# Layer B of a four-layer kernel: one accumulator bank per projection, the output product in four column quarters, the residual store behind the next step's first products

## The chip, the cores and the metric

The kernel runs on one core of one Trainium2 chip. The metric is the device time in microseconds (us) of one execution; "before" and "after" name the two kernels.

Words used throughout: TensorE (PE in the profile) multiplies, and each of its products is preceded by a weight load (PEld); VectorE (DVE), ScalarE (ACT) and GpSimd (POOL) work on elements; PSUM is the accumulator memory, which this program uses as eight banks of 512 float32 columns; SBUF is where the program keeps its other tiles. A *product* is one matmul instruction. Four products on four groups of 32 columns of the array run side by side (in the profile below, 20 products of 512 columns, five times four, take 1.07 us from start to start); I call four such a *round*. A *pass* is one whole output product of a step: 64 products before, 128 after.

## The reference

The program applies layers A, B, A, B to a sequence of 2048 tokens of width 640, each with a layer norm ahead and a residual add behind. Only B is changed. It is a recurrent transformer: 64 segments of 32 tokens, each with 8 memory tokens ahead of it, 32 heads of 128, and the memory of the next segment is the output of this one.

```python
mem = mem0
for s in range(64):
    h = concat([mem, x[:, 32*s : 32*s+32]])            # 8 + 32 tokens, 640 wide
    q, k, v = (einsum('btd,dhe->bhte', h, W) for W in (Wq, Wk, Wv))
    p = softmax(where(mask, q @ k.T * scale, -1e9))    # per head, 40 x 40
    o = einsum('bhte,hed->btd', p @ v, Wo)             # 4096 -> 640
    mem = o[:, :8]                                     # feeds the next segment
    outs.append(o[:, 8:])
```

So 64 steps form a chain: nothing of step s+1 that touches its memory tokens can start before the output product of step s has ended.

## The kernel before

The kernel skews the segments: a step handles rows 0 to 23 of segment s together with the 8 memory tokens of the next one; rows 24 to 31 of four segments (the "tails") are handled together, as filler work, and their output product is "deferred" to step 0 of the next four. So the steps repeat in cycles of four. The transposes between the products' layout (tokens on partitions) and that of the scores (features on partitions) are done by VectorE from PSUM.

The Q and K products of one half of the heads (16 of 32) share a two-bank tile; everything else takes one of four banks of a common pool:

```python
pp  = tile_pool(name="b_ps",  bufs=4, space=PSUM)     # one bank each
pot = tile_pool(name="b_pot", bufs=2, space=PSUM)     # two banks each

def qk(Wt, ps, b, dst):
    thin_mm(ps, cols, Wt, b, w_heads)                 # 5 chunks x 4 products, 512 columns
    tq = turn(ps)                                     # VectorE: 128x512 transpose to SBUF
    place("dve", tq, b, heads(dst[s]), 0, 8, 24)
    ...                                               # cut: GpSimd places the rest
# ... one step:
A_, B_ = pair_tile("b_QKa"), pair_tile("b_QKb")
qk(W.wq, A_[:, 0, :], 0, QT)
qk(W.wk, A_[:, 1, :], 0, KT)
qk(W.wq, B_[:, 0, :], 1, QT)
scores(0)
qk(W.wk, B_[:, 1, :], 1, KT)
...                                                   # cut: sums, normalise, V, values
```

The output product has 320 columns per product; the two halves of the width for two heads fill the four column groups, so the result has to be added across partitions afterwards, twice (for the next state and for the residual). Its end, and the end of the step:

```python
def run(self, k):                                     # class OPass
    if self.ps is None:
        self.ps = ps_tile([128, 320], F32, self.name)
    while k > 0 and self.p < 16:
        for e in range(2):
            h = self.horder[2 * self.p + e]
            for jj2 in range(2):
                q = 2 * e + jj2
                nc.tensor.matmul(self.ps[32*q:32*q+32, :], lhsT=self.src_fn(h),
                                 rhs=W.wo[:, h, 320*jj2:320*jj2+320], tile_position=(0, 32*q), ...)
...
fill(0.66); op.run(4); values(1); ...; op.run(4); fill(0.22); op.run(8)
...
nc.vector.transpose(out=TM, in_=ops[:])               # 128 x 320
for hf in range(2):                                   # two adds give the next state
    nc.vector.tensor_tensor(out=hT[s+1][64*hf:64*hf+64, :, 24:32],
        in0=TM[0:64, hf:10:2, 24:32], in1=TM[64:128, hf:10:2, 24:32], op=ALU.add)
fill(9)                                               # what is left of the filler
xo = add_out(ops, XO, "b_xnb")                        # two adds, 64 x 320, then the store
```

`fill` issues the filler products of the step: the tails (20 products of 512 columns per unit) in steps 1 to 3, the deferred output product in step 0.

Of the kernel before, what the change touches and what calls it, by code (L numbers as in the profile page):

```python
# [18 lines left out]
F32 = mybir.dt.float32  # L19
# [10 lines left out]
NCH = 5  # L30
# [28 lines left out]
def layernorm_tile(nc, pool, C, xt, xn_out, name):  # L59
# [8 lines left out]
    nc.vector.tensor_scalar(out=xn_out.rearrange("p (g jj d) -> p jj g d", jj=2, d=32),  # L68
                            in0=xt.rearrange("p (jj g d) -> p jj g d", jj=2, d=32),
# [497 lines left out]
def load_B_weights(nc, tc, ctx, B_Wq, B_Wk, B_Wv):  # L567
# [4 lines left out]
    for nm, src in (("wq", B_Wq), ("wk", B_Wk), ("wv", B_Wv)):  # L572
        t = wp.tile([128, NCH, 4096], BF16, name=f"b_{nm}")
        setattr(W, nm, t)
        sv = src.rearrange("(jj g d) h e -> g jj d (h e)", jj=2, d=32)
        for c in range(NCH):
            def load(t=t, sv=sv, c=c):
                for q in range(4):
                    nc.sync.dma_start(t[32 * q:32 * q + 32, c, :], sv[2 * c + q // 2, q % 2])
            loads.append(load)  # L580
# [3 lines left out]
def layer_B(nc, tc, C, W, wo_src, x_src, xb_src, x_dst, mem0, general, nsteps=64, out_bf16=False):  # L584
# [6 lines left out]
    with ExitStack() as ctx:  # L591
# [6 lines left out]
        pp = ctx.enter_context(tc.tile_pool(name="b_ps", bufs=4, space=PSUM))  # L598
# [18 lines left out]
        XO = st.tile([64, 320], F32, name="b_XO")  # L617
# [162 lines left out]
        class OPass:  # L780
            def __init__(self, src_fn, horder, name):
                self.src_fn, self.horder, self.name = src_fn, horder, name
# [3 lines left out]
            def run(self, k):  # L786
                if self.ps is None:
                    self.ps = ps_tile([128, 320], F32, self.name)
                while k > 0 and self.p < 16:
                    for e in range(2):  # L790
                        h = self.horder[2 * self.p + e]
                        for jj2 in range(2):
                            q = 2 * e + jj2
                            nc.tensor.matmul(self.ps[32 * q:32 * q + 32, :], lhsT=self.src_fn(h), rhs=W.wo[:, h, 320 * jj2:320 * jj2 + 320],
                                             start=(self.p == 0), stop=(self.p == 15), tile_position=(0, 32 * q), skip_group_check=True)
# [4 lines left out]
        def add_out(ops, XO, name):  # L800

            nc.vector.tensor_tensor(out=XO[0:64, :], in0=ops[0:64, :], in1=XO[0:64, :], op=ALU.add)
            if out_bf16:
                xnb = wk.tile([64, 320], BF16, name=name, tag="xnb")
                nc.vector.tensor_tensor(out=xnb[0:64, :], in0=ops[64:128, :], in1=XO[0:64, :], op=ALU.add)
                return xnb
            nc.vector.tensor_tensor(out=XO[0:64, :], in0=ops[64:128, :], in1=XO[0:64, :], op=ALU.add)
# [9 lines left out]
        for q in range(4):  # L817
# [3 lines left out]
        nc.vector.tensor_copy(m0[:, 1, :].rearrange("p (g jj d) -> p jj g d", jj=2, d=32),  # L821
                              m0[:, 0, :].rearrange("p (jj g d) -> p jj g d", jj=2, d=32))
# [18 lines left out]

        def load_deferred(T_):
            XOd[T_] = wk.tile([64, 320], F32, name="b_XOd", tag="XOd")
            for jj2 in range(2):
                for i in range(4):
                    r = 32 * (4 * T_ + i) + 24
                    nc.sync.dma_start(XOd[T_][32 * jj2 + 8 * i:32 * jj2 + 8 * i + 8, :], x_src[r:r + 8, 320 * jj2:320 * jj2 + 320])

        xn_pending = []
        for s in range(nsteps):  # L850
# [4 lines left out]
            for jj2 in range(2):  # L855
                nc.sync.dma_start(XO[32 * jj2:32 * jj2 + 24, :], x_src[32 * s:32 * s + 24, 320 * jj2:320 * jj2 + 320])
# [62 lines left out]
            def qk(Wt, ps, b, dst):  # L919

                thin_mm(ps, cols, Wt, b, w_heads)
                tq = turn(ps)
# [66 lines left out]
            A_, B_ = pair_tile("b_QKa"), pair_tile("b_QKb")  # L989
            qk(W.wq, A_[:, 0, :], 0, QT)  # L990
            qk(W.wk, A_[:, 1, :], 0, KT)
            qk(W.wq, B_[:, 0, :], 1, QT)
# [3 lines left out]
            qk(W.wk, B_[:, 1, :], 1, KT)  # L996
# [171 lines left out]
```

## Time and profile before

| | before |
|---|---|
| time, median (range) of 4 runs | 2796.89 us (2793.56 to 2800.34) |
| products on TensorE | 54,988, each with a weight load |
| one cycle of four steps in layer B | 62.3 us, 32 of them |
| TensorE's largest wait: first K for the transposed Q | 192.2 us |

The prediction below walks through the profile that leads there. Lines of the page of the kernel before give: busy time, share of the span and number of instructions of each engine; a DMA queue with the number of its packets, MB, and their share of the time of 16 engines; and a group of instructions (out<-in, shape, count | busy us, mean ns of one | idle before, and what ended most of it).

### The profile page before, as it was taken

The page shows a single profiled execution, that of the slowest core. Times are in us where ns is not written, and L with a number is a line of the kernel's source. Part 1 is how long each engine was busy: PE and PEld are TensorE (multiplying, and loading weights), DVE is VectorE, ACT ScalarE, POOL GpSimd, SP SyncE. Part 2 cuts the span into 40 slices and gives each one's busy share as a digit, 9 for nine tenths or more (in the row PEclk, how much of TensorE's full clock was granted, in tenths as well). Part 3 has the DMA queues.
Part 4 walks back from the last instruction along what each step waited for, and adds up shares of the span by engine and source line. Part 5 has one row for each costly group of instructions (what it writes and reads, how often), then busy time and mean ns, then how long its engine had stood idle before and what let it go on. Part 6 is the DMA issues. An engine that isn't in the chain of part 4 may idle for free.

```text
span 2796.9 us, 123979 instructions
## 1 busy us (share of the span) xinstructions
PE 2327.0 (83%) x54988; PEld 1285.9 (46%) x54988; DVE 1753.7 (63%) x4029; ACT 882.6 (32%) x2067; POOL 994.4 (36%) x2333
## 2 busy tenths in 40 slices
PE   6888878888888888888588887888888888888886
PEld 3444444444444444445344443444444444444443
DVE  5666656666666666666556665666666666666665
ACT  4665622222222222222156664222222222222221
POOL 2333433333333333333223433333333333333332
PEclk9988889999999999999889898999999999999999
DMA  6652330000000000000213324000000000000000
GB/s 170 162 150 84 110 96 21 19 21 19 21 22 20 20 20 22 19 18 18 68 55 121 114 81 159 18 17 17 18 18 17 17 18 17 20 18 17 15 16 13
DMA packets 98851, 131.87 MB, mean 47 GB/s; under 512 B 20592, under 2 KB 84096, under 8 KB 96384
## 3 DMA queue, kind: packets, MB, share of 16 engines
q1 hardware_dynamic: 96704, 122.20, 16.0%
q8 instruction: 432, 7.08, 1.1%
q10 hardware_dynamic: 1600, 1.66, 0.2%
q14 instruction: 115, 0.94, 0.1%
HBM read 89.17 MB, written 26.21 MB: 41 GB/s over the span
## 4 chain that ended last, share of the span: by engine, by line
PE 55%; DVE 19%; issue 7%; ACT 5%; DMA 2%; SPq 1%; POOL 1%; DVEq 0%; ACTq 0%; POOLq 0%
PE b_QKb L87 11%; PE b_V L87 10%; DVE b_TQ L87 9%; PE b_OPS L87 9%; PE b_QKa L87 8%; PE b_tail L87 3%; PE a_PP L87 3%; PE b_SP L87 3%; ACT a_PT L87 2%; PE b_OTL L87 2%; ACT b_OTsb L87 1%; PE a_S L87 1%; DVE b_TM L87 1%; ACT b_R L87 1%; DVE b_XO L87 1%
## 5 line engine op out<-in xcount | busy, mean ns | idle before, releaser
L87 PEld LDWEIGHTS <-b_hT 128*32 128x32 bf16 x15520 | 437.0, 98 | 644.6 <-issue 396.5
L87 ACT ACTIVATE b_PT<-b_SP 128x224 bf16<-128x224 f32 x256 | 91.5, 358 | 1098.5 <-PE b_SP L87 1089.7
L87 PE MATMUL b_OPS<-b_wo,b_OTsb 128*32 128x320 bf16 x8192 | 347.4, 301 | 17.2 <-ACT b_OTsb L87 13.1
L87 ACT ACTIVATE a_PT<-a_S 128x768 bf16<-128x768 f32 (+1 forms) x384 | 325.7, 891 | 84.9 <-PE a_S L87 77.9
L87 PE MATMUL b_QKa<-b_wk,b_hT 128*32 128x512 bf16 x2560 | 179.9, 413 | 192.2 <-DVE b_TQ L87 192.2
L87 PE MATMUL b_V<-b_wv,b_hT 128*32 128x512 bf16 x5120 | 325.0, 380 | 0.0
L87 DVE STREAM_TRANSPOSE b_TQ<-b_QKa 128x512 f32<-128x512 f32 x256 | 183.5, 717 | 193.3 <-PE b_QKa L87 190.6
L87 DVE STREAM_TRANSPOSE b_TQ<-b_QKb 128x512 f32<-128x512 f32 x256 | 183.5, 717 | 175.2 <-PE b_SP L87 116.0
L87 POOL CAST b_KT<-b_TQ 128x384 bf16<-128x384 f32 x254 | 142.7, 562 | 421.8 <-DVE b_TQ L87 421.8
L87 PEld LDWEIGHTS <-b_OTsb 128*32 128x32 bf16 x8192 | 187.1, 96 | 138.0 <-ACT b_OTsb L87 72.5
L87 POOL CAST b_QT<-b_TQ 128x384 bf16<-128x384 f32 x254 | 140.8, 554 | 297.4 <-DVE b_TQ L87 297.4
L87 DVE TENSOR_TENSOR b_PT<-b_PT,b_R 128x160 bf16<-128x160 bf16 (+1 forms) x512 | 215.0, 460 | 44.8 <-ACT b_R L87 44.4
L87 POOL TENSOR_TENSOR b_Rtot<-b_Rtot,b_R 128x160 bf16<-128x160 bf16 x256 | 142.8, 558 | 240.1 <-ACT b_R L87 224.5
L87 PE MATMUL b_QKb<-b_wk,b_hT 128*32 128x512 bf16 x2560 | 161.6, 380 | 50.2 <-DVE b_TQ L87 50.2
L87 PE MATMUL b_QKa<-b_wq,b_hT 128*32 128x512 bf16 x2560 | 162.9, 381 | 32.4 <-DVE b_hT L87 32.3
L87 POOL TENSOR_SCALAR_AFFINE_SELECT a_PT<-a_PT 128x256 bf16<-128x256 bf16 x256 | 109.6, 433 | 214.3 <-ACT a_PT L87 203.0
L87 ACT CAST b_OTsb<-b_OTL 128x320 bf16<-128x320 f32 x384 | 148.7, 421 | 114.5 <-PE b_OTL L87 114.4
L87 DVE CAST b_Vsb<-b_V 128x512 bf16<-128x512 f32 x256 | 174.4, 684 | 7.4 <-PE b_V L87 6.4
L87 PE MATMUL b_QKb<-b_wq,b_hT 128*32 128x512 bf16 x2560 | 175.0, 402 | 0.0
L87 PE MATMUL a_PP<-a_xnT,a_wt 128*128 128x512 bf16 x560 | 157.4, 417 | 2.7 <-DVE a_t1k L87 0.9
L87 ACT ACTIVATE b_R<-b_SP 128x160 f32<-128x160 f32 x256 | 78.1, 305 | 232.5 <-PE b_SP L87 232.5
L87 DVE STREAM_TRANSPOSE b_TM<-b_OPS 128x320 f32<-128x320 f32 x126 | 64.8, 514 | 137.4 <-PE b_OPS L87 137.4
(160 smaller groups left out, 3791.1 us busy)
## 6 DMA issues: line engine op xcount, KB each, us to landing
a_wt<-a_wpad SPq DMA_DIRECT2D x112, 160.0 KB
b_wo<-in_B_Wo_dram SPq DMA_DIRECT2D x8, 1280.0 KB
b_Vt<-b_Vtb SPq DMA_DIRECT2D x512, 16.0 KB
b_XO<-xres SPq DMA_DIRECT2D x256, 30.0 KB
a_wvo<-in_A_wo_dram SPq DMA_DIRECT2D x8, 800.0 KB
b_wq<-in_B_Wq_dram SPq DMA_DIRECT2D x20, 256.0 KB
b_wk<-in_B_Wk_dram SPq DMA_DIRECT2D x20, 256.0 KB
xres<-a_xo SPq DMA_DIRECT2D x16, 320.0 KB
```

The source lines that it names most:

```text
L87: r = f(*a, **k)
```

## The change

The intent: let the first products of a step follow each other without waiting for VectorE (a bank for every projection), shorten the chain from the output product to the next state (four column quarters need no add across partitions), and take the residual adds out of the way of the next step's first transpose. To pay for the banks, the common pool goes from four to three and the output product gets a bank of its own. The weights and the layer norm are laid out so that each column group gets one quarter of the width.

```diff
-        pp = tile_pool(name="b_ps", bufs=4, space=PSUM)
+        pp = tile_pool(name="b_ps", bufs=3, space=PSUM)
+        po = tile_pool(name="b_po", bufs=1, space=PSUM)
 class OPass:
-                    self.ps = ps_tile([128, 320], F32, self.name)
+                    self.ps = self.pool.tile([128, 160], F32, name=self.name, tag=self.tag)
-                        for jj2 in range(2):
-                            q = 2 * e + jj2
-                            matmul(self.ps[32*q:32*q+32, :], lhsT=src(h), rhs=W.wo[:, h, 320*jj2:320*jj2+320], ...)
+                        for q in range(4):
+                            matmul(self.ps[32*q:32*q+32, :], lhsT=src(h), rhs=W.wo[:, h, 160*q:160*q+160], ...)
 def add_out(ops, XO, name):                      # XO: [64, 320] -> [128, 160]
-            tensor_tensor(out=XO[0:64, :], in0=ops[0:64, :], in1=XO[0:64, :], op=ALU.add)
-                xnb = wk.tile([64, 320], BF16, name=name, tag="xnb")
-                tensor_tensor(out=xnb[0:64, :], in0=ops[64:128, :], in1=XO[0:64, :], op=ALU.add)
+                xnb = wk.tile([128, 160], BF16, name=name, tag=name)
+                tensor_tensor(out=xnb[:], in0=ops[:], in1=XO[:], op=ALU.add)
 # the step
-            A_, B_ = pair_tile("b_QKa"), pair_tile("b_QKb")
-            qk(W.wq, A_[:, 0, :], 0, QT)
-            qk(W.wk, A_[:, 1, :], 0, KT)
-            qk(W.wq, B_[:, 0, :], 1, QT)
+            qk(W.wq, "b_Qa", 0, QT)              # qk now takes a bank of the pool
+            qk(W.wk, "b_Ka", 0, KT)
+            while late: late.pop(0)()            # adds and stores of the step before
+            ... # cut: loads of the residual rows, moved here
+            qk(W.wq, "b_Qb", 1, QT)
-            fill(0.66)
+            fill(1.0)
             ...
-            fill(0.22)
-                TM = wk.tile([128, 10, 32], F32, ...)
-                for hf in range(2): tensor_tensor(out=hT[s+1][64*hf:...], ..., op=ALU.add)
+                TM = wk.tile([128, 5, 32], F32, ...)
+                tensor_copy(hT[s + 1][:, :, 24:32], TM[:, :, 24:32])
-            xo = add_out(ops, XO, "b_xnb"); ...  # store here
+            late.append(store)                   # the deferred output's store as well
```

Cut from it: the layout of the weights, the memory input and the layer norm's output, and the DMA lists that follow from the quarters.

More of the change, by code (lines that the diff above doesn't have):

```diff
@@ L67, in layernorm_tile @@
     nc.gpsimd.tensor_tensor(out=rstd[:], in0=rstd[:], in1=C.mhalf[:, 0:1], op=ALU.pow)
-    nc.vector.tensor_scalar(out=xn_out.rearrange("p (g jj d) -> p jj g d", jj=2, d=32),
-                            in0=xt.rearrange("p (jj g d) -> p jj g d", jj=2, d=32),
+    nc.vector.tensor_scalar(out=xn_out.rearrange("p (g q d) -> p q g d", q=4, d=32),
+                            in0=xt.rearrange("p (q g d) -> p q g d", q=4, d=32),
                             scalar1=mv[:, 0:1], scalar2=rstd[:, 0:1], op0=ALU.subtract, op1=ALU.mult)
@@ L574, in load_B_weights @@
         setattr(W, nm, t)
-        sv = src.rearrange("(jj g d) h e -> g jj d (h e)", jj=2, d=32)
+        sv = src.rearrange("(q g d) h e -> g q d (h e)", q=4, d=32)
         for c in range(NCH):
@@ L578, in load @@
                 for q in range(4):
-                    nc.sync.dma_start(t[32 * q:32 * q + 32, c, :], sv[2 * c + q // 2, q % 2])
+                    nc.sync.dma_start(t[32 * q:32 * q + 32, c, :], sv[c, q])
             loads.append(load)
@@ L597, in layer_B @@
         W.wo = wop.tile([128, 32, D], BF16, name="b_wo")
-        pp = ctx.enter_context(tc.tile_pool(name="b_ps", bufs=4, space=PSUM))
+        pp = ctx.enter_context(tc.tile_pool(name="b_ps", bufs=3, space=PSUM))
+        po = ctx.enter_context(tc.tile_pool(name="b_po", bufs=1, space=PSUM))
         pot = ctx.enter_context(tc.tile_pool(name="b_pot", bufs=2, space=PSUM))
@@ L616, in layer_B @@
             nc.vector.memset(Rtot[:], 0.0)
-        XO = st.tile([64, 320], F32, name="b_XO")
+        XO = st.tile([128, 160], F32, name="b_XO")
         nc.vector.memset(XO[:], 0.0)
@@ L780, in layer_B, with __init__ @@
         class OPass:
-            def __init__(self, src_fn, horder, name):
-                self.src_fn, self.horder, self.name = src_fn, horder, name
+            def __init__(self, src_fn, horder, name, pool=pp, tag="ps"):
+                self.src_fn, self.horder, self.name, self.pool, self.tag = src_fn, horder, name, pool, tag
                 self.ps = None
@@ L791, in run @@
                         h = self.horder[2 * self.p + e]
-                        for jj2 in range(2):
-                            q = 2 * e + jj2
-                            nc.tensor.matmul(self.ps[32 * q:32 * q + 32, :], lhsT=self.src_fn(h), rhs=W.wo[:, h, 320 * jj2:320 * jj2 + 320],
-                                             start=(self.p == 0), stop=(self.p == 15), tile_position=(0, 32 * q), skip_group_check=True)
+                        for q in range(4):
+                            nc.tensor.matmul(self.ps[32 * q:32 * q + 32, :], lhsT=self.src_fn(h), rhs=W.wo[:, h, 160 * q:160 * q + 160],
+                                             start=(self.p == 0 and e == 0), stop=(self.p == 15 and e == 1),
+                                             tile_position=(0, 32 * q), skip_group_check=True)
                     self.p += 1
@@ L800, in add_out @@
         def add_out(ops, XO, name):
-            nc.vector.tensor_tensor(out=XO[0:64, :], in0=ops[0:64, :], in1=XO[0:64, :], op=ALU.add)
             if out_bf16:
-                xnb = wk.tile([64, 320], BF16, name=name, tag="xnb")
-                nc.vector.tensor_tensor(out=xnb[0:64, :], in0=ops[64:128, :], in1=XO[0:64, :], op=ALU.add)
+                xnb = wk.tile([128, 160], BF16, name=name, tag=name)
+                nc.vector.tensor_tensor(out=xnb[:], in0=ops[:], in1=XO[:], op=ALU.add)
                 return xnb
-            nc.vector.tensor_tensor(out=XO[0:64, :], in0=ops[64:128, :], in1=XO[0:64, :], op=ALU.add)
+            nc.vector.tensor_tensor(out=XO[:], in0=ops[:], in1=XO[:], op=ALU.add)
             return XO
@@ L820, in layer_B @@
         alloc_h(0)
-        nc.vector.tensor_copy(m0[:, 1, :].rearrange("p (g jj d) -> p jj g d", jj=2, d=32),
-                              m0[:, 0, :].rearrange("p (jj g d) -> p jj g d", jj=2, d=32))
+        nc.vector.tensor_copy(m0[:, 1, :].rearrange("p (g q d) -> p q g d", q=4, d=32),
+                              m0[:, 0, :].rearrange("p (q g d) -> p q g d", q=4, d=32))
         mt = ps_tile([128, NCH, 8], BF16, "b_m0T")
@@ L840, in layer_B, with deferred_rows @@
         XOd = {}
+        def deferred_rows(x, T_, q):
+            v = x.rearrange("(t i k) d -> t i k d", i=4, k=32)
+            return v[T_, :, 24:32, 160 * q:160 * q + 160]
         def load_deferred(T_):
-            XOd[T_] = wk.tile([64, 320], F32, name="b_XOd", tag="XOd")
-            for jj2 in range(2):
-                for i in range(4):
-                    r = 32 * (4 * T_ + i) + 24
-                    nc.sync.dma_start(XOd[T_][32 * jj2 + 8 * i:32 * jj2 + 8 * i + 8, :], x_src[r:r + 8, 320 * jj2:320 * jj2 + 320])
+            XOd[T_] = wk.tile([128, 160], F32, name="b_XOd", tag="XOd")
+            for q in range(4):
+                nc.sync.dma_start(XOd[T_][32 * q:32 * q + 32, :], deferred_rows(x_src, T_, q))
         xn_pending = []
+        late = []
         for s in range(nsteps):
@@ L854, in layer_B @@
                 load_deferred(T - 1)
-            for jj2 in range(2):
-                nc.sync.dma_start(XO[32 * jj2:32 * jj2 + 24, :], x_src[32 * s:32 * s + 24, 320 * jj2:320 * jj2 + 320])
             if not last:
@@ L917, in row_max, with qk @@
                 mrows.append(mr)
-            def qk(Wt, ps, b, dst):
+            def qk(Wt, name, b, dst):
+                ps = ps_tile([128, 512], F32, name)
                 thin_mm(ps, cols, Wt, b, w_heads)
-                tq = turn(ps)
+                tq = turn(ps[:])
                 place("dve", tq, b, heads(dst[s]), 0, 8, 24)
@@ L987, in take, with vpass @@
                 evac(eng, OTsb[:, h:h + 8, :].rearrange("p (j r) c -> p j (r c)", j=2), OTL[b, jp][:, :, 0:160])
-            A_, B_ = pair_tile("b_QKa"), pair_tile("b_QKb")
-            qk(W.wq, A_[:, 0, :], 0, QT)
-            qk(W.wk, A_[:, 1, :], 0, KT)
-            qk(W.wq, B_[:, 0, :], 1, QT)
+            def vpass(b):
+                V = ps_tile([128, 512], F32, "b_V")
+                thin_mm(V, vcols, W.wv, b, w_cols)
+                evac("dve", Vsb[:, b, :], V[:])
+            qk(W.wq, "b_Qa", 0, QT)
+            qk(W.wk, "b_Ka", 0, KT)
+            while late:
+                late.pop(0)()
+            for q in range(4):
+                nc.sync.dma_start(XO[32 * q:32 * q + 24, :], x_src[32 * s:32 * s + 24, 160 * q:160 * q + 160])
+            qk(W.wq, "b_Qb", 1, QT)
             if general:
@@ L995, in layer_B @@
             scores(0)
-            qk(W.wk, B_[:, 1, :], 1, KT)
+            qk(W.wk, "b_Kb", 1, KT)
             while xn_pending:
@@ L1004, in layer_B @@
                 row_max(1)
-            Va = ps_tile([128, 512], F32, "b_V")
-            thin_mm(Va, vcols, W.wv, 0, w_cols)
-            evac("dve", Vsb[:, 0, :], Va[:])
+            vpass(0)
             scores(1)
-            Vb = ps_tile([128, 512], F32, "b_V")
-            thin_mm(Vb, vcols, W.wv, 1, w_cols)
-            evac("dve", Vsb[:, 1, :], Vb[:])
+            vpass(1)
             sums(1)
@@ L1018, in layer_B @@
                 tails_to_seg(s + 1)
-            fill(0.66)
-            op = OPass(lambda h: OTsb[:, h, 0:32], HORDER, "b_OPS")
+            fill(1.0)
+            op = OPass(lambda h: OTsb[:, h, 0:32], HORDER, "b_OPS", po, "op")
             op.run(4)
@@ L1041, in layer_B @@
             if not last:
-                TM = wk.tile([128, 10, 32], F32, name="b_TM", tag="TM")
+                TM = wk.tile([128, NCH, 32], F32, name="b_TM", tag="TM")
                 nc.vector.transpose(out=TM[:].rearrange("p g t -> p (g t)"), in_=ops[:])
-                for hf in range(2):
-                    nc.vector.tensor_tensor(out=hT[s + 1][64 * hf:64 * hf + 64, :, 24:32], in0=TM[0:64, hf:10:2, 24:32],
-                                            in1=TM[64:128, hf:10:2, 24:32], op=ALU.add)
+                nc.vector.tensor_copy(hT[s + 1][:, :, 24:32], TM[:, :, 24:32])
             fill(9)
@@ L1051, in layer_B, with store @@
                 ln_dma((s + 7) // 4)
-            xo = add_out(ops, XO, "b_xnb")
-            for jj2 in range(2):
-                nc.sync.dma_start(x_dst[32 * s:32 * s + 24, 320 * jj2:320 * jj2 + 320], xo[32 * jj2:32 * jj2 + 24, :])
+            def store(s=s, ops=ops):
+                xo = add_out(ops, XO, "b_xnb")
+                for q in range(4):
+                    nc.sync.dma_start(x_dst[32 * s:32 * s + 24, 160 * q:160 * q + 160], xo[32 * q:32 * q + 24, :])
+            late.append(store)
             def store_deferred(T_, od):
@@ L1059, in store_deferred @@
                 xd = add_out(od.ps, XOd.pop(T_), "b_xnbd")
-                for i in range(4):
-                    for jj2 in range(2):
-                        r = 32 * (4 * T_ + i) + 24
-                        nc.sync.dma_start(x_dst[r:r + 8, 320 * jj2:320 * jj2 + 320], xd[32 * jj2 + 8 * i:32 * jj2 + 8 * i + 8, :])
+                for q in range(4):
+                    nc.sync.dma_start(deferred_rows(x_dst, T_, q), xd[32 * q:32 * q + 32, :])
             for u in units:
                 if isinstance(u, OPass):
-                    store_deferred(T - 1, u)
+                    late.append(lambda u=u, T=T: store_deferred(T - 1, u))
             if last:
+                while late:
+                    late.pop(0)()
                 od = deferred.pop(T)
```

## The prediction

(Cut from the text, each cut marked: rules of the hardware that did not come from this case's traces. No term of the sum goes with them: 2796 - 214 - 22 - 20 = 2540 us still stands, on times of the trace before. Without them the 69 ns of a round of 160 columns is an estimate from that trace: 512 columns in 214 ns scale to 67, the 224 columns of b_blk in 0.10 us to 71. Measured later: 69 ns in the kernel after; a round of 320 columns, 135.5 in the text, takes 136 before. That makes 2.21 us per pass against 2.18, so the 0.04 per step, 0.2 in the sum of a cycle, is as fine as these readings go. That Q can be transposed while K's products run was the author's reading, not shown by the trace before; the kernel after shows it, see "Right" below.)

> **What bounds the kernel now.** I first read the page. Its chain of waits puts over half of the span on TensorE and a fifth on VectorE, nearly all in layer B (tiles b_...), and part 5 names the largest wait of TensorE: 192.2 us ahead of the K product of the first half of the heads, until VectorE's transposed copy b_TQ is done. Both products lie in one two-bank tile, b_QKa.
>
> ```profile
> PE 55%; DVE 19%; issue 7%; ACT 5%; DMA 2%; SPq 1%; POOL 1%; DVEq 0%; ACTq 0%; POOLq 0%
> ...
> L87 PE MATMUL b_OPS<-b_wo,b_OTsb 128*32 128x320 bf16 x8192 | 347.4, 301 | 17.2 <-ACT b_OTsb L87 13.1
> ...
> L87 PE MATMUL b_QKa<-b_wk,b_hT 128*32 128x512 bf16 x2560 | 179.9, 413 | 192.2 <-DVE b_TQ L87 192.2
> ...
> L87 PE MATMUL b_QKb<-b_wk,b_hT 128*32 128x512 bf16 x2560 | 161.6, 380 | 50.2 <-DVE b_TQ L87 50.2
> ```
>
> Layer B runs 64 steps, twice. The starts of the Q product in the timeline repeat every four steps (0: the filler is the deferred output product; 1, 2, 3: V, Q, K tails; a layer norm ends step 2, its transposes lie in step 3). So I asked for the stretches of one cycle:
>
> ```profile
> 813.68:829.23 15.55, 13.26 (x404) 8.07 (x404) 10.33 (x23) 3.25 (x11) 6.71 (x16) 1.00 0.07 17
> 829.23:844.39 15.16, 13.31 (x385) 7.38 (x373) 10.01 (x23) 3.83 (x12) 5.89 (x15) 1.00 0.12 27
> 844.39:860.12 15.73, 13.43 (x380) 7.44 (x377) 10.87 (x26) 3.83 (x12) 5.06 (x11) 1.00 0.07 16
> 860.12:876.00 15.88, 13.76 (x381) 7.53 (x382) 10.12 (x23) 3.84 (x12) 5.63 (x12) 1.00 0.10 24
> sum 62.32, PE 53.76 PEld 30.42 DVE 41.33 ACT 14.75 POOL 23.28; mean PE 13.44 PEld 7.61 DVE 10.33 ACT 3.69 POOL 5.82
> ```
>
> Columns: length, then busy TensorE, weight loads, VectorE, ScalarE, GpSimd, granted clock. No engine fills a step; VectorE is at two thirds. TensorE is the in-order path, and its holes make the step. Its timeline at the head of step 1:
>
> ```profile
> 829.23 1.25 PE L87 MATMUL b_QKa<-b_wq,b_hT 128*32 128x512 bf16 x20
> 831.83 1.26 PE L87 MATMUL b_QKa<-b_wk,b_hT 128*32 128x512 bf16 x20 [1.34 <-DVE b_TQ L87]
> 832.90 1.26 PE L87 MATMUL b_QKb<-b_wq,b_hT 128*32 128x512 bf16 x20
> 833.98 0.26 PE L87 MATMUL b_SP<-b_mask,c_identb 128*32 128x160 bf16 x4
> 834.33 0.37 PE L87 MATMUL b_SP<-b_QT,b_KT 128*32 128x40 bf16 x32
> 835.06 1.26 PE L87 MATMUL b_QKb<-b_wk,b_hT 128*32 128x512 bf16 x20 [0.36 <-DVE b_TQ L87]
> 836.13 0.29 PE L87 MATMUL b_SP<-b_PT,b_blk 128*32 128x160 bf16 x8
> 836.23 1.27 PE L87 MATMUL b_V<-b_wv,b_hT 128*32 128x512 bf16 x20
> ```
>
> Unblocked, a product starts 1.07 us after its predecessor (831.83 to 832.90). Before the first K there are 2.60 - 1.07 = 1.5 us of hole. VectorE starts a transpose 1.38 us after a product starts, if it is free; here it first does the output adds of the last step, so Q is transposed only at 831.06.
>
> The second layer B has one thing more, in step 1. VectorE's timeline there:
>
> ```profile
> 2089.71 0.48 DVE L87 TENSOR_TENSOR b_XOd<-b_OPSd,b_XOd 64x320 f32<-64x320 f32 x1
> 2091.57 0.49 DVE L87 TENSOR_TENSOR b_xnbd<-b_OPSd,b_XOd 64x320 bf16<-64x320 f32 x1 [1.38 <-DMA out_dram<-b_xnb]
> 2092.09 0.72 DVE L87 STREAM_TRANSPOSE b_TQ<-b_QKa 128x512 f32<-128x512 f32 x1
> ```
>
> The two output tiles share one buffer, so the add waits for a store and the Q transpose waits behind it.
>
> [...] Q and K lie in different banks of the pair, so I read the 1.5 us as a wait of the tile's bookkeeping, not of the chip; this kernel never overlaps the two, so its trace cannot show it. [...] 20 products of 512 columns in 1.07 us are 5 rounds of 214 ns. [...] the window 2092.86 to 2096.27, behind a hole of 2.9 us, has a granted clock of 0.59. [...] The row-sum products b_blk (one round of 160 columns, one of 64) take 0.10 us (836.13 to 836.23)[...]. So 160-column rounds should stream at about 69 ns.
>
> **The change part by part.**
> Own banks: the first K starts behind Q. Holes removed in steps 0 to 3, from starts in the timeline less 1.08 us: 1.81, 1.52, 1.07, 1.82 = 6.2. The second K needs no transpose any more either: 0.5 us per step (835.06 - 834.33 - 0.22 for the scores), 2.0 per cycle. Sum 8.2.
>
> Scores of the first half still need K transposed and placed: K starts at 1.08, transpose at 2.46 to 3.18, cast (0.23) to 3.44, scores at 3.6, against 3.3 when TensorE could: 0.3, as now.
>
> Output product in quarters: 128 products instead of 64, half as long: 32 x 69 = 2.21 us against 16 x 135.5 = 2.17. Cost 0.04 per step.
>
> The chain to the next step gets shorter: transpose 128x320 (517 ns; 512 columns take 717, so some 1.05 ns per column) becomes 128x160, about 350; two adds of 196 become one copy of about 200. So 0.35 less. Outside step 2 the five filler rounds left (1.08 us) cover the chain (estimate 0.9 us) and nothing is gained; in step 2 the layer norm makes VectorE late and the gain is about 0.4.
>
> Filler moved forward: the first output product now waits 0.25 us for b_OTsb (step 2); two more filler parts (0.43) cover it. Gain 0.25 per step, 1.0 per cycle. But the filler part before the last output products is gone, and b_OTsb comes 1.06 us after the values start while 0.84 of work is left: loss 0.22 per step, 0.9 per cycle.
>
> Store moved behind K: adds of 4 x 0.48 us at worst leave the Q transpose's way and become one of about 0.33 (two in step 1), in front of the transpose of the second Q.
>
> Three single banks instead of four: I took from the built program which instruction each bank wait names. Two of them bite. In step 3 the first V waits for the transpose of the second K, since the layer norm's transposes took a bank: about 0.7. In step 1 the second K waits for the deferred add: about 0.4. The values wait for V's copy, which starts behind normalising: about 0.2 more per step, 0.8 per cycle.
>
> Sum per cycle: 8.2 + 1.0 + 0.4 gained; 0.2 + 0.9 + 0.7 + 0.4 + 0.8 lost: 6.6. Laying the instructions of each step one after another by hand gives 13.4, 13.75, 14.3, 14.1, together 55.6 against 62.3, so 6.7. Times 32 cycles: 214 us.
>
> Second layer B, step 1: 16.5 instead of 15.15 us where the clock stays up, because of the shared buffer; the names are separate now: 16 x 1.35 = 22 us. The slow-clock windows add to the steps they fall in some 10 us in the first layer B (6 steps of about 17.4 instead of 15.9) and 16 us in the second (step 1 at 17.9 instead of 16.5). With the long holes gone I expect most to go: 20 us.
>
> 2796 - 214 - 22 - 20 = 2540 us. Layers A are not touched.
>
> **The rivals.** *Output product bound by issue*: if rounds of 160 columns took 100 ns, 160 passes (128 and 32 deferred) of 32 rounds would cost 31 ns each, 160 us, and leave about 2700. Against it: the 0.10 us of b_blk, and scores rounds of about 27 ns. *Banks become the wait*: three banks, one more transpose waiting for each; were every V to wait for a transpose by 0.7 us, 90 us, about 2630. For: the bank waits in the build; against: most name work that ends a microsecond before. *VectorE takes over*: 10.3 us busy per step, about 9.2 after (adds 0.6, transposes and copies 0.35 less), in a 13.9 us step: no bound, but its order shows in the waits. *The wait only moves*: the recurrence from output to next state limits the step, so removing the K hole helps only as far as scores(0) come earlier. They do: from 5.1 us into step 1 to 3.6, and nothing behind them is late.
>
> **Range and chances.** My hand-laid cycle can be off by 1.5 us (48 us) either way; clock windows by 25. That gives 2490 to 2610; a rival at full size lies outside. Faster by over 2% means under 2740, which only a rival of 200 us prevents: 0.95. Same 0.04, slower 0.01.
>
> **What would show it.** The wait of the first K on b_TQ (192.2) gone, that of the second K below 20; steps of 13.3 to 14.4; b_OPS at about 180 to 190 ns per product and 2.2 us per pass; b_TM near 350 ns; V waiting for b_TQ in step 3 only; granted clock near 1.0 in both layers B. I am wrong if the output pass takes over 2.6 us, if V or Q waits for a bank in every step, or if the hole reappears ahead of the scores.

## More of the kernel before

```profile
PE 2327.0 (83%) x54988; PEld 1285.9 (46%) x54988; DVE 1753.7 (63%) x4029; ACT 882.6 (32%) x2067; POOL 994.4 (36%) x2333
...
q8 instruction: 432, 7.08, 1.1%
...
L87 DVE STREAM_TRANSPOSE b_TM<-b_OPS 128x320 f32<-128x320 f32 x126 | 64.8, 514 | 137.4 <-PE b_OPS L87 137.4
```

The middle line is the one that I passed over: I take it to be the transfer of TensorE's own instructions. Every packet of that queue has 16,384 bytes, and (54,988 + 54,988) / 432 = 254.6, so one packet holds about 255 products and loads.

## The result, and the profile after

| | before | after |
|---|---|---|
| median of 4 runs | 2796.89 us | 2650.07 us |
| lowest to highest | 2793.56 to 2800.34 | 2642.03 to 2653.92 |

All outputs are right. The ratio is 0.9472, with a 95% interval of 0.9454 to 0.9491. The kernel is faster by 5.3%, but 110 us slower than predicted and outside the range of 2490 to 2610.

The page of the kernel after:

```profile
PE 2301.3 (87%) x65166; PEld 1440.4 (54%) x65228; DVE 1600.3 (60%) x3743; ACT 882.3 (33%) x2067; POOL 992.5 (38%) x2333
...
q8 instruction: 512, 8.39, 1.4%
...
PE 70%; DVE 8%; issue 8%; ACT 3%; POOL 2%; DMA 1%; SPq 0%; DVEq 0%; POOLq 0%; ACTq 0%
...
L87 PE MATMUL b_OPS<-b_wo,b_OTsb 128*32 128x160 bf16 x16384 | 365.8, 234 | 58.9 <-issue 50.9
...
L87 PE MATMUL b_Ka<-b_wk,b_hT 128*32 128x512 bf16 x2560 | 170.6, 383 | 0.1
...
L87 PE MATMUL b_Kb<-b_wk,b_hT 128*32 128x512 bf16 x2560 | 163.1, 379 | 3.1 <-DVE b_xnbd L87 2.2
...
L87 DVE STREAM_TRANSPOSE b_TM<-b_OPS 128x160 f32<-128x160 f32 x126 | 43.7, 347 | 187.2 <-PE b_OPS L87 187.0
```

What was to go is gone: the first K waits 0.1 us instead of 192.2 and the second 3.1 instead of 50.2; VectorE's share of the chain falls from 19% to 8%. But the output product, which waited 17.2 us before, mostly for ScalarE, now waits 58.9 us, and 50.9 of that for "issue": time in which the engine waited for nothing that the profile shows. In the chain line "issue" grows only from 7% to 8%, so that line alone does not give the cause away. The waits of TensorE in the kernel after do (engine and tile <- releaser: total us, times, longest); before had no such entry for any product of layer B:

```profile
PE b_OPS L87 <- issue: 50.9, 68, 1.5
...
PE b_OPSd L87 <- issue: 26.6, 22, 1.7
...
PE b_OTL L87 <- issue: 18.3, 24, 1.6
PE b_tail L87 <- issue: 12.1, 16, 1.6
```

With three smaller ones (b_Qa 9.7, b_SP 6.3, b_V 2.7) they sum to 126.6 us. They do not belong to one product: whatever comes next in the queue gets the hole, and each hole is at most 1.7 us long. One cycle of the first layer B after, step by step, in the columns of the prediction:

```profile
779.96:795.26 15.30, 13.26 (x527) 9.47 (x531) 7.83 (x18) 3.25 (x11) 6.17 (x15) 1.00 0.08 18
795.26:808.81 13.55, 13.34 (x453) 8.96 (x445) 8.23 (x19) 3.83 (x12) 5.87 (x15) 1.00 0.11 26
808.81:823.29 14.48, 13.70 (x446) 8.98 (x440) 10.42 (x24) 3.83 (x12) 5.67 (x12) 1.00 0.11 22
823.29:837.20 13.91, 13.53 (x448) 8.77 (x449) 9.23 (x20) 3.84 (x12) 5.61 (x12) 1.00 0.12 28
sum 57.24, PE 53.83 PEld 36.19 DVE 35.71 ACT 14.75 POOL 23.33; mean PE 13.46 PEld 9.05 DVE 8.93 ACT 3.69 POOL 5.83
```

Steps 1 to 3 are near the 13.75, 14.3 and 14.1 laid by hand. Step 0, predicted as the shortest (13.4), is the longest, 15.3; its products rose from 404 to 527. The steps are irregular, too: over the first layer B, step 0 takes 14.6 to 16.7 us. The medians of the four steps sum to 58.4 us where 55.6 was predicted; 2.8 x 32 = 90 us of the 110.

TensorE's timeline at the end of that step 0 (start, busy us, how many, and in brackets the idle time ahead):

```profile
789.89 0.73 PE L87 MATMUL b_OPS<-b_wo,b_OTsb 128*32 128x160 bf16 x31
791.49 1.35 PE L87 MATMUL b_OPS<-b_wo,b_OTsb 128*32 128x160 bf16 x65 [0.86 <-issue]
792.61 1.28 PE L87 MATMUL b_OPSd<-b_wo,b_OTdef 128*32 128x160 bf16 x63
794.98 0.52 PE L87 MATMUL b_OPSd<-b_wo,b_OTdef 128*32 128x160 bf16 x17 [1.08 <-issue]
```

The holes fall in the middle of a product whose operands have long been there. Between the two stand 65 + 63 = 128 products with as many weight loads: 256 instructions, just one packet of the instruction queue.

### The profile page after: what moved, and what is told of

The parts are those of the page before. It is cut to its first block, busy times and chain, and to the rows that moved or that the text cites. A ratio compares the mean times of both kernels' runs of the same rounds, so it can differ in the third digit from the quotient of the medians. Undisturbed runs are those within 1.5% of the kernel's fastest.

```text
span 2645.6 us, 144539 instructions
## 1 busy us (share of the span) xinstructions
PE 2301.3 (87%) x65166; PEld 1440.4 (54%) x65228; DVE 1600.3 (60%) x3743; ACT 882.3 (33%) x2067; POOL 992.5 (38%) x2333
## 3 DMA queue, kind: packets, MB, share of 16 engines
q1 hardware_dynamic: 116160, 122.21, 17.6%
## 4 chain that ended last, share of the span: by engine, by line
PE 70%; DVE 8%; issue 8%; ACT 3%; POOL 2%; DMA 1%; SPq 0%; DVEq 0%; POOLq 0%; ACTq 0%
PE b_OPS L87 12%; PE b_V L87 11%; PE b_tail L87 8%; PE b_Qa L87 6%; PE b_Ka L87 5%; PE b_Kb L87 5%; PE b_SP L87 4%; PE b_Qb L87 4%; PE b_OTL L87 3%; PE b_OPSd L87 3%; PE a_PP L87 3%; ACT a_PT L87 2%; DVE b_TQ L87 2%; PE a_S L87 2%; DVE a_qk L87 1%
## 5 line engine op out<-in xcount | busy, mean ns | idle before, releaser
L87 PE MATMUL b_OPS<-b_wo,b_OTsb 128*32 128x160 bf16 x16384 | 365.8, 234 | 58.9 <-issue 50.9
L87 PEld LDWEIGHTS <-b_OTsb 128*32 128x32 bf16 x16384 | 289.2, 97 | 120.3 <-issue 68.3
L87 DVE STREAM_TRANSPOSE b_TQ<-b_Qa 128x512 f32<-128x512 f32 x128 | 91.8, 717 | 206.8 <-PE b_Qa L87 204.8
L87 PE MATMUL b_Qa<-b_wq,b_hT 128*32 128x512 bf16 x2560 | 172.5, 381 | 21.0 <-DVE b_hT L87 10.0
L87 PE MATMUL b_Ka<-b_wk,b_hT 128*32 128x512 bf16 x2560 | 170.6, 383 | 0.1
L87 PE MATMUL b_Qb<-b_wq,b_hT 128*32 128x512 bf16 x2560 | 168.1, 380 | 0.0
L87 PE MATMUL b_Kb<-b_wk,b_hT 128*32 128x512 bf16 x2560 | 163.1, 379 | 3.1 <-DVE b_xnbd L87 2.2
L87 DVE STREAM_TRANSPOSE b_TM<-b_OPS 128x160 f32<-128x160 f32 x126 | 43.7, 347 | 187.2 <-PE b_OPS L87 187.0
L87 PE MATMUL a_S<-a_qk 32*128 32x512 bf16 (+3 forms) x1024 | 143.9, 323 | 7.1 <-ACT a_PT L87 5.8
L87 PEld LDWEIGHTS <-b_hx 128*32 128x32 bf16 x3840 | 101.2, 97 | 85.6 <-issue 25.1
```

What stands on the lines that cost most here:

```text
L87: r = f(*a, **k)
```

## The experiments

**Theory F (fetch): TensorE runs out of instructions.** The quarters double the products of the output product; they stream as fast as I thought (69 ns per round), but, as I read the traces, TensorE's instructions arrive in packets of about 255 (the kernel after has 2 x 10,240 more products and loads than before in 80 more packets, 256 in each), no faster than one packet in about 3.5 us, and where 255 instructions are used up sooner, TensorE stands. Numbering all products, weight loads and semaphore instructions of TensorE in order, the holes of each layer B lie at one position modulo 256. In the trace after, starts of products over 0.3 us apart lie within eight neighbouring positions 109 times in the first layer B and 91 times in the second, together 184 us with the work that lies in them; in the trace before no position stands out, and the fullest eight hold about 20 in each layer. (The expectations below use an earlier count of mine, 183 and 19 us.)

**The packets in time.** From the records of the queue after: TensorE resumes 2.56 us (median) after a packet's transfer starts, and the next transfer starts 1.2 us after it resumes. Holes in a row lie 3.75 us apart in the first layer B (median; at least 3.47), and no two transfers started closer than 3.36 us before and 3.17 after. So the working figure, an estimate from these, is 3.5 us per 255 instructions. (The expectations below put that spacing at 3.4 and 3.65 us, earlier estimates; a block of 256 there is a packet here.)

**What a packet lasts.** Start to start, measured on products four apart, a round of 160 columns takes 69 ns (median), one of 320 columns 136. A round is 8 instructions, a packet 32 rounds. As an estimate from these: 32 x 69 ns = 2.2 us with quarters, below 3.5; 32 x 136 = 4.4 with halves, above; 32 x 214 = 6.8 for 512 columns. One step holds 440 products with quarters and 376 with halves; step 0 528 and 400, of them 256 quarters nearly in a row.

**Rivals.** *S, streaming*: short products cost more than their columns, whatever the fetch does. *B, banks*: three banks instead of four make TensorE wait, and the profile hides it as issue. *V, VectorE*: the late adds get in the way. A fourth, that the data transfers of the change (19,456 more packets on queue q1, for the quarters' rows) slow the fetch, got no run of its own; against it speaks that a packet of instructions took 1.11 us after and 1.07 before (medians), and that the holes grew below where the number of instructions alone grew.

### The output product back in halves

Everything of the change but the quarters: own banks, three-bank pool, late stores and filler split stay; the layouts, two adds and two-piece stores return. (The deferred bf16 result takes the buffer of the normalised rows.)

```diff
-  self.ps = self.pool.tile([128, 160], ...);  for q in range(4): ... rhs=W.wo[:, h, 160*q:160*q+160]
+  self.ps = self.pool.tile([128, 320], ...);  for jj2 in range(2): ... rhs=W.wo[:, h, 320*jj2:320*jj2+320]
+  # and with it: XO [64, 320], TM [128, 10, 32] with two adds, weights as before
```

> The changed kernel with only the output products taken back to two column halves (64 instead of 128 per pass, same columns; the sum with the residual is again two adds). Theory F (TensorE's instructions come in blocks of 256, a block takes at least 3.4 us to arrive, and the quarters use blocks up faster): the holes at block boundaries in both layers B fall from 183 us to under 40, and the time falls below the changed kernel's 2650 although the chain to the next state and the late adds get longer: 2570 to 2630. Rival B (the three single banks make the waits that are missing in my sum): nothing gained, 2660 to 2700.

Measured: 2568.21 us (2567.37 to 2569.6), ratio to before 0.9178 [0.9162, 0.9193]. Undoing the quarters makes it 82 us faster, just below the 2570 to 2630 us expected. TensorE's waits in this kernel (three entries):

```profile
PE b_Kb L87 <- DVE b_XOd L87: 22.5, 15, 1.5
PE b_Kb L87 <- DVE b_xnbd L87: 22.5, 15, 1.5
...
PE b_OTL L87 <- issue: 0.2, 1, 0.2
```

"Issue" has fallen from 126.6 us in the products of layer B to 0.2, and the instruction queue has 432 packets again. Rivals B and V fall as the cause: their parts are all still here. In exchange the second K waits 45 us for a bank that the deferred product's adds, now two and late, hold.

### The kernel before with quarters alone

```diff
 # on before
-  [128, 320] output tile, two halves, two adds
+  [128, 160] output tile, four quarters, one copy to the next state, one add to the residual
+  # with it, as in the kernel after: the two bf16 results in buffers of their own
```

> The kernel before with only the output products in four quarters. Theory F: steps are long enough (about 15.6 us against 3.5 blocks of 3.65 us), so most holes at block boundaries fall into waits that are there anyway, but some are left: shorter adds and chain gain some 30 us, boundary holes cost as much or more: 2760 to 2830, with boundary holes of 60 us or more in the layers B where the kernel before has 19. Rival B: a gain of 30 to 60 us, no boundary holes.

Measured: 2797.0 us (2791.28 to 2799.81), ratio 0.9989 [0.9973, 1.0006]: the same. TensorE's waits:

```profile
PE b_QKa L87 <- DVE b_TQ L87: 113.5, 128, 0.9
PE b_OPS L87 <- issue: 44.9, 71, 1.5
PE b_QKb L87 <- DVE b_TQ L87: 44.9, 128, 0.6
PE b_OPSd L87 <- issue: 33.2, 26, 1.6
```

This is a useful null: the time did not move, yet two things did. The shorter chain and the single add cut the first K's wait from 192.2 to 113.5 us, 79 us (some of it may come from the separate buffers, whose sharing cost VectorE 21.9 us before); issue holes in all of layer B's products, about 95 us, took it back. The quarters are good for VectorE and bad for TensorE's supply.

### More instructions, same columns

F says that the count does it, S that short rounds do. So the tails of the kernel after, which are not part of the change, are cut in two pieces of 256 columns: 40 more products per step in three of four steps, and not one column more.

```diff
 def thin_parts(...):                      # tails only
-    matmul(ps[32*j:32*j+32, :], lhsT=cols(c), rhs=wsel(Wt, c, b, j), ...)
+    for n in range(2):
+        matmul(ps[32*j:32*j+32, 256*n:256*n+256], lhsT=cols(c), rhs=<256 columns of it>, ...)
```

> The changed kernel with each tail product of 512 columns cut into two of 256: 40 more pairs of weight load and product in three of four steps, no more columns. Theory F: 40 pairs are 0.31 block, at 3.65 us each 1.1 us in 90 steps, so about 60 to 110 us more: 2710 to 2760. Rival (columns count, not instructions):[...] 2645 to 2660.

(From the runs, two rounds of 160 columns take 138 ns where one of 320 takes 136; as an estimate from that, 2 ns for each of ten more rounds in 90 steps are about 2 us, which leaves the rival's range as it is.)

Measured: 2721.78 us (2720.8 to 2727.94), ratio 0.9726: 72 us more than after. From its page and its waits:

```profile
q8 instruction: 542, 8.88, 1.4%
```

```profile
PE b_OPS L87 <- issue: 96.9, 113, 1.6
PE b_tail L87 <- issue: 36.8, 33, 1.6
PE b_OPSd L87 <- issue: 27.5, 21, 1.6
PE b_OTL L87 <- issue: 18.4, 25, 1.6
```

Thirty packets more (with q1's 116,160 data packets as in the kernel after), and the holes grow most ahead of b_OPS, whose products are the same as in the kernel after (50.9 to 96.9 us). That is not a price of short rounds. As an estimate, a packet of uncut tail products lasts 6.8 us (32 x 214 ns), of tails cut in two about half as long, near the 3.5 us between packets: the long tails had left the supply time that it no longer has. All issue waits in layer B's products sum to about 201 us, 74 more than after, against 72 us of time. The counterpart, the same edit where there is slack, comes last.

### Only the deferred product in halves

```diff
 # on after: the deferred output product alone
-  160-column quarters
+  320-column halves, its own [64, 320] residual rows, two adds
```

> The changed kernel with only the deferred output product (one step in four) in halves: 64 pairs less in that step, two adds more in the next. Theory F: that step falls from about 15.7 to about 14.3 us, the next grows by up to 0.6: 2600 to 2635. Rival B: no gain or a loss from the adds, 2650 to 2670.

Measured: 2605.82 us (2604.44 to 2613.0), ratio 0.9321 [0.9305, 0.9337]: 44 us less than after. Waits:

```profile
PE b_OPS L87 <- issue: 41.6, 71, 1.3
PE b_tail L87 <- issue: 14.3, 21, 1.3
...
PE b_OPSd L87 <- issue: 0.4, 1, 0.4
```

Half of the 82 us with a fifth of the quarters (32 of 160 passes), because the deferred product stands beside the output product of step 0, where the two form a run of 256 short products: the median step 0 goes from 15.7 to 14.1 us. (The next step grew from 14.0 to 15.1 us, more than the 0.6 expected, so that the time shows less than the holes do.) All issue waits now sum to about 67 us. So it is the density of a stretch that counts, not the total.

### Halves, with the deferred add at its old place

On the halves kernel, the 45 us that the second K waits for the deferred adds are taken away by moving that store back to the end of the step.

```diff
-                    late.append(lambda u=u, T=T: store_deferred(T - 1, u))
+                    store_deferred(T - 1, u)
```

> e1_halves with the add and store of the deferred product (one step in four) left where the kernel before has it, at the end of its step; only the step's own store stays behind the next K. In e1_halves the second K of the next step waits 45 us in total for that add, which holds the bank. Theory: the add fits into VectorE's idle time before the first transpose, step 1 falls from 14.9 to about 13.5 us, total 2520 to 2535. Rival (VectorE's order delays the first transpose instead): 2555 to 2575.

Measured: 2524.86 us (2522.82 to 2525.9), ratio 0.9023 [0.9008, 0.9038]. One cycle:

```profile
700.52:713.72 13.20, 13.10 (x400) 8.14 (x401) 9.53 (x21) 3.24 (x11) 6.11 (x15) 1.00 0.09 19
713.72:727.09 13.37, 13.18 (x385) 7.44 (x378) 9.97 (x22) 3.87 (x13) 5.88 (x15) 1.00 0.13 29
727.09:741.53 14.44, 13.19 (x377) 7.56 (x377) 11.53 (x27) 3.78 (x12) 5.67 (x12) 1.00 0.09 19
741.53:755.75 14.22, 13.71 (x382) 7.88 (x382) 9.79 (x22) 3.84 (x12) 5.53 (x12) 1.00 0.10 27
sum 55.23, PE 53.18 PEld 31.02 DVE 40.82 ACT 14.73 POOL 23.18; mean PE 13.29 PEld 7.75 DVE 10.20 ACT 3.68 POOL 5.80
```

55.23 us against 55.6 laid by hand for the kernel after, and 13.20, 13.37, 14.44, 14.22 against 13.4, 13.75, 14.3, 14.1. TensorE is busy all but 0.1 us of step 0. It is not the same kernel, since its transpose is the longer one of 320 columns, but its order on TensorE is the one that I had laid out: without the fetch holes that cycle exists.

### Which parts carry the gain

On that kernel, three parts are undone one by one.

```diff
 # no late store: the residual adds at the end of their own step
-            late.append(store)
+            store()
 # no own banks: Q and K in the two-bank tiles of before, the rest unchanged
-            qk(W.wq, "b_Qa", 0, QT); qk(W.wk, "b_Ka", 0, KT) ...
+            A_, B_ = pair_tile("b_QKa"), pair_tile("b_QKb"); qk(W.wq, A_[:, 0, :], 0, QT) ...
 # old filler split
-            fill(1.0) ... op.run(4); op.run(8)
+            fill(0.66) ... op.run(4); fill(0.22); op.run(8)
```

> e1_halves with both stores back at the end of their step, as in the kernel before. If moving the store behind K matters, the two adds delay the first transposes, and with them the scores, by about 0.5 us in the steps that follow a transpose of a tail: 20 to 60 us more than the kernel with only the deferred store early (2520 to 2535 expected), so 2545 to 2590. If it doesn't matter: the same as that kernel within 8 us.

Measured: 2529.27 us (2528.4 to 2531.2), ratio 0.904. The late store is worth at most 4 us there (0.2%, no more than runs of one kernel differ), the case "it doesn't matter" of the expectation: this part of the change brought next to nothing. This kernel also gives the cleanest reading of the banks: from the kernel before it differs in own banks, pools, filler split and separate bf16 buffers, and it is 268 us faster.

> The kernel with halves and the deferred store early, but Q and K back in two-bank tiles. If the banks carry the gain, the hole before the first K (1.07 us at least) and before the second K (0.5) come back in all 128 steps: 150 to 200 us more than the same kernel with own banks, so 2670 to 2735. If the late store or the filler carried it: less than 60 us more.

Measured: 2813.87 us (2811.97 to 2815.28), ratio 1.0054: the own banks are worth 289 us there, together with what their absence does to the late store, and without them the kernel is no better than before. I expected 2670 to 2735 and missed, so here is why, from the groups on its page:

```profile
L87 PE MATMUL b_QKa<-b_wk,b_hT 128*32 128x512 bf16 x2560 | 166.8, 390 | 112.1 <-DVE b_TQ L87 112.1
...
L87 PE MATMUL b_QKb<-b_wk,b_hT 128*32 128x512 bf16 x2560 | 161.6, 380 | 151.5 <-DVE b_TQ L87 151.5
```

The late residual add is in VectorE's order between the transposes of the first K and the second Q. With shared tiles the second K waits for exactly that transpose, 151.5 us instead of 50.2 in the kernel before. The late store helps only where no product waits for the next transpose; the parts of this change do not add up one by one.

> The kernel with halves and the deferred store early, with the filler split as in the kernel before (0.66 and 0.22 instead of 1.0). By my sum 0.25 us per step lost and 0.22 won: within 12 us of the same kernel with the new split.

Measured: 2519.53 us (2518.12 to 2522.4), ratio 0.9006. The new filler split costs 5 us (0.2%) if anything; it is no gain.

### Beyond the change

With the old filler split, the longest step is step 2, at whose end VectorE computes a layer norm while TensorE waits for the next state (b_Qa for b_hT, 31.5 us). So its statistics are moved one step ahead, and the load of its rows with them; and then its transposes in step 3 are put into the output product's bank, because they had taken one of the three and made the first V wait for a transpose (6.9 us, 28 times).

```diff
 # first kernel: step 1 computes mean and variance, step 2 only applies them (ends of the conditions cut)
-            if s % 4 == 1: ln_dma((s + 7) // 4)
+            if s % 4 == 0: ln_dma((s + 8) // 4)
+            if s % 4 == 1: ln_stats((s + 7) // 4)
 # second kernel: as well
-            tps = ps_tile([128, NCH, 128], BF16, "b_lntps")
+            tps = po.tile([128, NCH, 128], BF16, name="b_lntps", tag="op")
```

> The fastest so far (halves, own banks, deferred store early, old split of the filler: 2519.5 us) with the statistics of the layer norm moved from the end of step 2 to VectorE's idle time at the end of step 1. The norm keeps the next state waiting in step 2 (about 1 us over the other steps): 2485 to 2505; if VectorE has no room there either: 2515 to 2530.

> The same, and the layer norm's transposes in the output product's bank instead of one of the three single banks, so that the first V of step 3 waits for no transpose: step 3 from 14.1 to about 13.5 us, 15 to 25 us less than the kernel with early statistics; 0 if the V is held by something else.

Measured: 2492.71 us (2491.78 to 2496.24), ratio 0.892, and 2478.34 us (2476.4 to 2479.91), ratio 0.8866 [0.8852, 0.8881]. The waits that the two edits aim at, first without them, then with the first:

```profile
PE b_Qa L87 <- DVE b_hT L87: 31.5, 34, 1.2
...
PE b_Qa L105 <- DVE b_hT L105: 7.1, 6, 1.2
PE b_V L105 <- DVE b_TQ L105: 6.9, 28, 0.5
```

With both edits, b_V's wait for the transpose is no longer listed. The median step 2 fell from 14.26 to 13.24 us, then step 3 from 14.12 to 13.57. (The 14 us of the second edit are just below the 15 to 25 expected, and more than the 6.9 us of that one wait; the rest I did not take apart.) The last kernel beats both the kernel before (by 11.3%) and the kernel after (by 172 us of the medians), and uses halves.

### The split tails where there is slack

The same 40 extra products per step as above, but on the halves kernel with 2524.86 us.

> The kernel with halves and the deferred store early (2525 us) with the tail products cut in two: the edit that cost 72 us on the changed kernel. Theory F: now a cycle has about 1650 pairs, 12.9 blocks, 47 us at 3.65 us each against 55 us of steps, so blocks mostly arrive in time: 0 to 30 us more. If cutting the products had cost by itself (columns, overhead): the same 72 us.

Measured: 2547.31 us (2545.3 to 2548.31), ratio 0.9109: 22 us more, where the same edit cost 72 on the kernel with quarters. Its largest issue wait:

```profile
PE b_OPS L87 <- issue: 8.3, 20, 1.1
```

All its issue waits in layer B sum to about 15 us. Rival S would charge the same price for the same products in both kernels; it could explain at most the 22. The 50 us that are left of the 72 go with the supply, since columns and products of the edit are the same. This settles between the two.

## Why the prediction was right or wrong

**Right: what bounded the kernel before.** The first K's wait on the transposed Q is gone (192.2 to 0.1 us), the second's is 3.1, below the 20 named. The own banks carry the gain: 268 us between the kernel before and the one with halves and both stores at their old places, where their term was 8.2 x 32 = 262. In step 1 of the cycle after, the scores start 3.62 us into the step, as worked out (3.6):

```profile
795.26 1.31 PE L87 MATMUL b_Qa<-b_wq,b_hT 128*32 128x512 bf16 x20
796.34 1.31 PE L87 MATMUL b_Ka<-b_wk,b_hT 128*32 128x512 bf16 x20
...
798.88 0.37 PE L87 MATMUL b_SP<-b_QT,b_KT 128*32 128x40 bf16 x32
```

The second product starts 1.08 us behind the first, with no bracket of idle time. VectorE transposes Q from 796.68 to 797.40 us, while K's products run into another bank, and the result is right: so what the prediction read without being able to show it, that the 1.5 us were not a wait of the chip, held in this kernel.

**Right: the short terms.** The transpose of the output takes 347 ns (about 350 predicted), the copy to the next state 183 (about 200), the residual add 325 (about 330). The first V waits 7.9 us for a transpose, 28 times, where I had 0.7 x 32 = 22; the second K waits for the deferred add only 2.2 us in all, 9 times, where I had 0.4 per cycle: both smaller. The first Q waits for the next state 10.0 us in all instead of 32.3, 0.7 per cycle where I had 0.4. VectorE's wait for the store from the shared buffer (21.9 us, 16 times before) is gone. The granted clock in the layers B went from 0.99 and 0.98 to 1.00 and 1.00, and its stretches at half clock from 19 to 3; the 20 us were not measured by themselves. The filler split, balanced at 1.0 us won and 0.9 lost per cycle, loses at most 5 us in a run: about nothing, as worked out.

**Wrong: the step "Output product in quarters ... Cost 0.04 per step".** Its stream time was right: a round starts 69 ns after the last. What it left out is the supply of instructions: 64 more products per pass, with as many weight loads, in 160 passes: 10,240 more of each in the whole program. (The pages show 10,240 more loads and 10,178 more products; some records of products are missing.) Measured, that is 126.6 us of issue holes, more than the whole miss of 110 us. Whether all of it would come off the time is not shown, since no kernel has quarters without the holes: splitting the tails added 74 us of holes and 72 us of time, but the deferred product in halves took away 60 us of holes and 44 us of time. Net, with the rest of the change left as it is, the quarters cost 82 us (2650.07 - 2568.21), since they do shorten VectorE's work (the transpose of the output from 514 to 347 ns); moving the deferred store early as well gives 2524.86 us, inside the range that I had predicted, but by a different kernel.

**Wrong: the rival "Output product bound by issue" was dismissed.** I named it, with about 2700 us for it at full size, and then set it aside for two reasons: b_blk's 0.10 us and score rounds of 27 ns. Both are true and neither bears on it. b_blk is 8 products and one half's scores 32, that is 16 and 64 instructions, well within one packet of 255. A burst shows how fast instructions can start, not how fast they can be supplied. The evidence that would have told lay in the same trace: the packets of the instruction queue, never closer than 3.36 us, and 512 instructions of step 0's two output products due in 128 products x 2 / 4 x 69 ns = 4.4 us, where two packets need about 7.

**A check that was badly built.** I had named "b_OPS at about 180 to 190 ns per product"; the record says 234, with rounds of 69 ns all the same. A record is about 165 ns longer than the round that it belongs to (234 against 69 ns after, 301 against 136 before), so its mean does not tell the rate; starts do. The other check, "the output pass takes over 2.6 us", was the right one, and it fired: in the timeline above 96 of the 128 products of a pass take from 789.89 to 792.61 us, 2.72 us, with a hole of 0.86 us inside.

**Smaller slips, which do not bear on the miss.** The 48 and 25 us either way that the range rests on would give 2467 to 2613, not 2490 to 2610. VectorE's 10.3 us less 0.6 and 0.35 is 9.35, not 9.2 (one cycle after: 8.93). What the trace before shows: 17 stretches at half clock of 3.41 us each lie inside the layers B, and in the 3.41 us ahead of each TensorE had been busy for 0.7 to 1.3 us. In the trace after it is one. (The 19 and 3 above count two more each at the edge of the second layer B.) What sets off such a stretch is not shown.

**What stays open.** That TensorE stands for want of a packet is read from the times of transfers and holes, not shown directly; nor is it known why the next transfer starts only 1.2 us after TensorE resumes, or why TensorE resumes only 2.56 us after a transfer starts, when the transfer takes 1.11. Whether the fetch itself could be made earlier, or packed work placed between so that quarters pay, was not tried. The 3.5 us are this program's, on one core.

## What to carry to other kernels

Cutting a product into shorter ones cost more here than its columns, 82 us (2650.07 - 2568.21): check that a packet's worth of instructions (here about 128 products with their loads) lasts longer than its supply takes (here about 3.5 us, the estimate above), over the densest stretch and not on average. The sign here was an idle time named "issue", 126.6 us in holes of at most 1.7, that fell ahead of whatever product came next and returned at one position modulo 256; count instructions of an engine and packets of its instruction queue before and after. When a rival is dismissed by a measurement, check that the measurement lasts long enough for the rival to show.
